# Attention and two MoE layers in one kernel: masked scores to SBUF, exponential in place, and another price list for the operation planner

## The chip, the cores and the metric

The kernel runs on one core of one Trainium2 chip. The metric is the device time of one execution in microseconds (us); the median of three runs stands for a kernel. Engines are named as in the profile: PE is the tensor engine, PEld its weight loads, DVE the vector engine, ACT the scalar engine, POOL is GpSimd, SP the queue that issues most DMAs.

## The reference

Everything is fp32. Attention has 4 batches, 8 heads, 576 positions and head size 64; its result becomes 2304 tokens of width 512 and passes through two MoE-like layers.

```
scores = q @ k^T / 8;  decay[i,j] = cum[i] - cum[j],  cum = cumsum(log(clip(f)))
s = where(j > i, -1e9, scores + decay);  s -= max(s)
attn = exp(s);  attn /= sum(attn) + 1e-9;  x = attn @ v        # 2304 x 512
h = x @ w1_in (512 x 2048);  x = (h * sigmoid(1.702 h)) @ w1_out
h = x @ w2_in;               out = (max(h,0) + alpha*min(h,0)) @ w2_out
```

## The kernel before

Every matmul operand is split into a high and a low fp32r half, so that a product takes three matmuls. The work is cut into operations ("ops"), and the kernel does not issue them in the order of the source: `plan.add` records an op with the engines it may use and what each would cost, and `Plan.plan` then simulates the whole kernel with those costs and picks, step by step, the op that could start first. [...]

**The planner's rules for PE.** Each PE op has a `mode`, meant to be the form in which the 128x128 array is used. An op whose mode differs from the one before it is charged `SWITCH` ns. When candidates are compared, an op of another mode counts as starting `pen` ns later than it could, unless it has been ready for `hold_for` ns already; ops of the first MoE product ("gemm1", `back`, priority 1000 and above) count as starting at least `back` ns later. `TRIES` lists the triples (pen, hold_for, back); each is planned and the plan with the earliest last start is used. `LAT` (230 ns) is added between engines. `pad` puts filler matmuls (L484) where the plan leaves PE idle in the first 130 us.

**The attention.** There are 16 pairs of heads (4 batches, 4 pairs each). A pair has two chunks of queries, 0 to 255 and 256 to 575. `chunk` computes a chunk's scores: for each tile of 128 queries and each head one PSUM bank, filled by matmuls with 64 rows (L878, mode 1; the two heads share the array), and for the last 64 queries of both heads by full-array matmuls (L872, mode 0). A DVE pass (L891, with a read of its accumulator) adds the mask, scales by -1/8 and takes the row minimum; an ACT pass (L900) takes the exponential and its row sum. Then come a small add (L909 or L905), the reciprocal (L911) and the scaling of the row (`a_scale`, L919 on DVE or POOL, L917 on ACT). `chunk2` transposes the scaled rows on PE by 128x128 blocks against the identity (L952), copies them out of PSUM (L513 ACT, L515 DVE, tiles `eT`) and multiplies by v (L966, half the array's columns per head, mode 2). `chunk2` of a chunk is added after `chunk` of the next one.

Per head pair there are ten passes L891 and ten exponentials, 160 of each in all: for each of the row lengths 128, 256, 288, 384 and 512, 32 of them.

**Buffers.** Eight PSUM banks are shared; scores may hold 3 at a time, the transposes 3, the v products 1, gemm1 2, the loads' transposes 2. In SBUF the rows of a tile lie in `ea`, `eb`, `ec`, `ed` (views `view[t, i]`, two buffers each), the transposed rows in `eT` (`ET` buffers of 640 columns), a pair's q in `QA` (`QS` buffers of two times 576).

**What runs beside it.** Once a block of tokens is finished, its share of gemm1 (L1008) can fill PE at low priority; what is left of it runs after the attention. Later come a tail of gemm1 in a seven-product scheme (L1031), the second product (L1252), and the second layer (the same scheme, L1434).

Of the kernel before, what the change touches and what calls it, by code (L numbers as in the profile page):

```python
# [23 lines left out]
QLAG = 3000.0  # L24
QPRI = 109.0
SLAG = 1000.0
SWITCH = 105.0
TMODE = 2
PADC = 8000.0
PAD0, PAD1, PADN, PADM = 1600.0, 130000.0, 220.0, 200.0  # L30
TRIES = [(60.0, 600.0, 400.0), (60.0, 300.0, 400.0)]
QUEUE = {"SP": "SP", "ACTQ": "ACT"}


# [215 lines left out]
def kernel(  # L250
# [45 lines left out]
    KEPT = 4  # L296
    HF = 256

    EB, ET, QS = 2, 4, 3
    SC_D, SC_A, SC_P = 0.0, 0.0, 0.0  # L300
    A0 = 100.0
    plan = Plan()
# [196 lines left out]
    def c_dve(n, fast=False):  # L499
        return n / (1.92 if fast else 0.96) + 68.0  # L500
# [206 lines left out]
    def load_qk(src, b, h0, w, c0, pri, actq):  # L707

        raw, T = Buf(p_raw), Buf(p_tk)
        for o in range(0, P, 32):  # L710
            hh, e_ = o // 64, o // 32 % 2
            d_ = DMA(32 * w * 4 * 1.6)
            if actq:
                d_.append(("ACTQ", d_[0][1], 300.0))
            plan.add(d_, lambda e, hh=hh, e_=e_, o=o: E[e].dma_start(
                raw.ap[o:o + 32, 0:w].rearrange("p (n d) -> p n d", d=32),
                src[b, h0 + hh, c0:c0 + w, 32 * e_:32 * e_ + 32].rearrange("(n p) d -> p n d", p=32),
            ), (), [(raw, o)], pri, QLAG if pri < QPRI else 0.0)
        plan.add([("DVE", 1.25 * w + 85.0)], lambda e: nc.vector.transpose(T.ap[:, :w], raw.ap[:, :w]), [raw], [T], pri)  # L719
        return T  # L720

    def split(T, w, big, keys, pri):
# [108 lines left out]
        return max(n / 2.4 + 13.5, 111.0 if m > 64 else 57.0)  # L831

    def a_scale(n):
        return [("DVE", c_dve(n, True), SC_D, True), ("ACT", c_act(n) + 30.0, SC_A), ("POOL", 280.0 + 2.55 * n, SC_P, True)]

    def chunk(u, q0, q1, pri):
        kh, kl, dk, qh, ql, qo, z = (u[x] for x in ("kh", "kl", "dk", "qh", "ql", "qo", "z"))
        pr = lambda c: range(2 if c > SPLIT else 1)
        ms = Buf(p_ms)
        n = q1 - q0  # L840
        tiles = [(t, t * P, min(P, S - t * P)) for t in range(q0 // P, (q1 + P - 1) // P)]
        view, eb = {}, {}
        if not q0:
            e0 = Buf(p_e0)
        for j, (t, a, w) in enumerate(tiles):
            ext = a + w
            if not q0:
                eb[t] = e0
                for hh in range(2):
                    view[t, hh] = lambda c0, c1, o=2 * P * j + hh * ext: e0.ap[:, o + c0:o + c1]  # L850
            elif w == P:
                eb[t] = x = Buf((p_e2, p_e3)[j])
                for hh in range(2):
                    view[t, hh] = lambda c0, c1, x=x, hh=hh: x.ap[:, hh, c0:c1]
            else:
                eb[t] = x = Buf(p_e4)
                fe = filled("ed", p_e4)
                view[t, 0] = lambda c0, c1, x=x: x.ap[:, c0:c1]
            step = ext if ext <= 512 else ext // 2
            for c0 in range(0, ext, step):  # L860
                c1 = c0 + step
                if q0 or j == 0:
                    pms = [Buf(ps_s) for _ in range(2 if w == P else 1)]
                f0 = 0 if q0 else a

                def mm(e, pms=pms, a=a, w=w, c0=c0, c1=c1, f0=f0):
                    if w < P:
                        o = pms[0].ap[:, :c1 - c0]
                        zz = lambda i: z.ap[:, i].rearrange("p h c -> p (h c)")
                        l = [(zz(0), kh.ap[:, c0:c1]), (zz(0), kl.ap[:, c0:c1]), (zz(1), kh.ap[:, c0:c1]), (ones[:, 1], dk.ap[:, c0:c1])]  # L870
                        for i, (x, y) in enumerate(l):
                            nc.tensor.matmul(o, x, y, start=i == 0, stop=i == 3)  # L872
                        return
                    for i, (x, y) in enumerate(((qh, kh), (qh, kl), (ql, kh), (None, dk))):
                        for hh in range(2):
                            r = slice(64 * hh, 64 * hh + 64)
                            l = ones[r, 0, :w] if x is None else x.ap[r, a - qo:a - qo + w]
                            nc.tensor.matmul(pms[hh].ap[:, f0:f0 + c1 - c0], l, y.ap[r, c0:c1], start=i == 0, stop=i == 3, skip_group_check=True)  # L878

                rd = [*((x, p_) for x in (kh, kl) for p_ in pr(c1)), *((dk, (i, p_)) for i in range(2) for p_ in (range(2) if u["first"] else pr(c1))), b_one, *u["fdk"]]  # L880
                rd += [z] if w < P else [qh, ql]
                plan.add([("PE", (4.4 if w == P else 4.0) * c_mm(c1 - c0, P))], mm, rd, [(x, f0) for x in pms], pri, mode=1 if w == P else 0,
                    pad=(pms[0], lambda x=pms[0], f0=f0, n=min(P, c1 - c0): x.ap[:, f0:f0 + n], 4 if pri == A0 and j == 0 else 0))
                for i, pm in enumerate(pms):
                    col = 4 + (c0 > 0) if w < P else 2 * j + i
                    if w == P:
                        mk, m0 = mask, 3 * P - t * P + c0
                    else:
                        mk, m0 = (mask, 0) if c1 < ext else (mask2, 0)
                    first = (lambda col=col: ms.ap[:, col - 1:col]) if c0 else lambda: 1.0e38  # L890
                    plan.add([("DVE", c_dve(c1 - c0) + 20.0)], lambda e, pm=pm, c0=c0, c1=c1, mk=mk, m0=m0, col=col, f0=f0, first=first: nc.vector.tensor_tensor_reduce(  # L891
                        pm.ap[:, f0:f0 + c1 - c0], pm.ap[:, f0:f0 + c1 - c0], mk[:, m0:m0 + c1 - c0], -0.125, first(),
                        ALU.add, ALU.min, accum_out=ms.ap[:, col:col + 1],
                    ), [b_mask if mk is mask else b_mask2, *([(ms, ("m", col - 1))] if c0 else [])], [(pm, f0), (ms, ("m", col))], pri)
                    if w == P:
                        last.append((pm, t, i, 0, c1, f0, col, 6 + col))
                    else:
                        last.append((pm, t, 0, c0, c1, f0, 5, 10 + (c0 > 0)))
            for pm, t_, i, x0, x1, f0, mc, sc in last:
                plan.add([("ACT", c_act(x1 - x0, True) + 190.0)], lambda e, pm=pm, t_=t_, i=i, x0=x0, x1=x1, f0=f0, mc=mc, sc=sc: nc.scalar.activation(  # L900
                    view[t_, i](x0, x1), pm.ap[:, f0:f0 + x1 - x0], AF.Exp, scale=-1.0, bias=ms.ap[:, mc:mc + 1], accum_out=ms.ap[:, sc:sc + 1]
                ), [(pm, f0), (ms, ("m", mc)), *(fe if w < P else [])], [(eb[t_], (t_, i, x0)), (ms, ("s", sc))], pri)
            last.clear()
            if w < P:
                plan.add([("DVE", 75.0, 0.0, True)], lambda e: nc.vector.scalar_tensor_tensor(  # L905
                    ms.ap[:, 10:11], ms.ap[:, 10:11], 1e-9, ms.ap[:, 11:12], op0=ALU.add, op1=ALU.add
                ), [(ms, ("s", 11))], [(ms, ("s", 10))], pri)
            else:
                plan.add([("DVE", 70.0, 0.0, True)], lambda e, j=j: nc.vector.tensor_scalar_add(ms.ap[:, 6 + 2 * j:8 + 2 * j], ms.ap[:, 6 + 2 * j:8 + 2 * j], 1e-9), (), [(ms, ("s", 6 + 2 * j)), (ms, ("s", 7 + 2 * j))], pri)  # L909
            cs = [6 + 2 * j, 7 + 2 * j] if w == P else [10]  # L910
            plan.add([("DVE", 85.0)], lambda e, cs=cs: nc.vector.reciprocal(ms.ap[:, cs[0]:cs[-1] + 1], ms.ap[:, cs[0]:cs[-1] + 1]), (), [(ms, ("s", c)) for c in cs], pri)  # L911
            for i, c in enumerate(cs):
                ks = [(eb[t], (t, i, x)) for x in range(0, ext, step)]
                def sc_(e, t=t, i=i, c=c, ext=ext):
                    x = view[t, i](0, ext)
                    if e == "ACT":
                        nc.scalar.mul(x, x, ms.ap[:, c:c + 1])  # L917
                    else:
                        E[e].tensor_scalar_mul(x, x, ms.ap[:, c:c + 1])  # L919
                plan.add(a_scale(ext), sc_, [(ms, ("s", c))], ks, pri)  # L920
        return dict(u=u, q0=q0, q1=q1, pri=pri, view=view, eb=eb)
# [3 lines left out]
    def chunk2(x):  # L925
# [5 lines left out]
        for t in range(nt):  # L931
# [27 lines left out]
            def av(e, et=et, t=t, s0=s0, m=m, w=w):  # L959
# [9 lines left out]
                    )  # L969
                    seen.add(hh)  # L970

            plan.add([("PE", max(4 * m / 2.4, 230.0) + 30.0)], av, [vr, et, *u["fvr"]], [pb], pri, mode=2,
                pad=(pb, lambda: pb.ap[:, :P], 0) if t == 0 else None)
        t0 = col0(b, q0)
        x = t0
# [530 lines left out]
```

## Time and profile before

| | |
|---|---|
| median of 3 runs | 969.73 us (969.11 to 970.33) |
| the profiled execution | 968.71 us, its span 967.0 us |
| PE busy over the span | 98% |
| DVE, ACT, POOL busy | 77%, 58%, 5% |
| granted TensorE clock | 0.999 of full speed |
| attention stretch | about the first 300 us |

The span runs from the first to the last instruction; 1.71 us of the execution's own time lie around it. The busy share of PE contains time in which matmuls are in flight but none is issued, so 98% is not 98% of its peak. Shares of busy time are averages over stages with different limits.

### The profile page before, as it was taken

What the parts mean: (1) busy time and instruction counts of PE and PEld (TensorE: products, weight loads), DVE (VectorE), ACT (ScalarE), POOL (GpSimd) and SP (SyncE); (2) the same over time, 40 slices, a digit from 0 to 9 for tenths busy, and PEclk for the clock granted to TensorE, in tenths of its full rate; (3) what the DMA queues carried; (4) which work ended last, traced back from release to release, by engine and by line L of the source; (5) the groups of instructions that cost most, each with busy time, mean ns of one, the idle gap of its engine ahead of it and who ended that gap; (6) DMA issues with size and microseconds to landing.
All of it is one profiled execution on the core that took longest, in us unless ns stands there. A gap on an engine that the chain in (4) does not pass through costs nothing.

```text
span 967.0 us, 18109 instructions
## 1 busy us (share of the span) xinstructions
PE 948.4 (98%) x6513; PEld 870.1 (90%) x6513; DVE 747.4 (77%) x1759; ACT 564.7 (58%) x1240; POOL 46.8 (5%) x56
## 2 busy tenths in 40 slices
PE   8999999999999999999999999999999999999998
PEld 5788887778889999988888988999999999999998
DVE  5999988888758029937657895888668978988987
ACT  6998977666564247757667784566455733221212
POOL 1112101010000003100000000000000000000000
PEclk9999999999999999999999999999999999999999
DMA  7868563432112247757887685678729495453523
GB/s 148 181 177 199 159 159 77 80 77 64 55 36 87 89 151 221 226 165 258 304 307 273 218 267 180 227 289 288 283 103 341 153 388 184 142 153 109 153 77 99
DMA packets 179035, 172.78 MB, mean 179 GB/s; under 512 B 98320, under 2 KB 153760, under 8 KB 176640
## 3 DMA queue, kind: packets, MB, share of 16 engines
q1 hardware_dynamic: 178928, 171.61, 57.3%
q8 instruction: 51, 0.84, 0.4%
q14 instruction: 40, 0.33, 0.1%
q10 hardware_dynamic: 16, 0.01, 0.0%
HBM read 107.71 MB, written 63.85 MB: 177 GB/s over the span
## 4 chain that ended last, share of the span: by engine, by line
PE 84%; DVE 11%; ACT 2%; DMA 2%; issue 1%; SPq 1%; DVEq 0%; ACTq 0%
PE bk L1031 23%; PE bk L1252 20%; PE bk L1434 19%; PE bk L1008 10%; PE bk L966 4%; PE bk L878 3%; DVE bk L891 3%; PE bk L952 3%; PE bk L872 2%; DVE ea L919 1%; DVE ec L919 1%; ACT ea L900 1%; DVE eT L515 1%; DVE tk L719 1%; DVE wc L688 1%
## 5 line engine op out<-in xcount | busy, mean ns | idle before, releaser
L1031 PE MATMUL bk<-x,wS 128*128 128x384 f32 x912 | 160.5, 335 | 0.3 <-DVE lx L1057 0.3
L1031 PEld LDWEIGHTS bk<-x,wS 128*128 128x128 f32 x912 | 158.1, 188 | 1.1 <-DVE lx L1057 0.8
L1252 PE MATMUL bk<-lh,w 128*128 128x512 f32 (+1 forms) x640 | 146.8, 368 | 0.0
L1008 PE MATMUL bk<-xh,w 128*128 128x320 f32 (+2 forms) x640 | 145.2, 307 | 0.2 <-DVE w L518 0.2
L1252 PEld LDWEIGHTS bk<-lh,w 128*128 128x128 f32 x640 | 112.8, 189 | 19.9
L1008 PEld LDWEIGHTS bk<-xh,w 128*128 128x128 f32 x640 | 108.3, 189 | 4.9 <-issue 2.6
L1008 PE MATMUL bk<-xl,w 128*128 128x320 f32 (+2 forms) x320 | 97.0, 303 | 0.0
L518 DVE TENSOR_TENSOR ll<-lx,lh 128x512 fp32r<-128x512 f32 (+1 forms) x80 | 50.9, 636 | 49.8 <-PE bk L1252 41.6
L1252 PE MATMUL bk<-ll,w 128*128 128x512 f32 (+1 forms) x320 | 81.2, 368 | 0.0
L891 DVE CUSTOM_DVE_ANT_0 bk<-bk,mask 128x128 f32<-128x128 f32 (+4 forms) x144 | 68.1, 498 | 16.6 <-PE bk L878 13.7
L513 ACT CAST x<-x 128x768 fp32r<-128x768 f32 (+3 forms) x41 | 33.4, 825 | 67.7 <-PE bk L1434 55.2
L1434 PE MATMUL bk<-wS,x 128*128 128x256 f32 x567 | 70.5, 283 | 0.0
L1434 PEld LDWEIGHTS bk<-wS,x 128*128 128x128 f32 x567 | 69.1, 192 | 0.0
L1434 PE MATMUL bk<-wS,lh 128*128 128x256 f32 x378 | 68.7, 283 | 0.0
L1218 ACT ACTIVATE lx<-lx 128x512 f32<-128x512 f32 (+1 forms) x80 | 46.9, 587 | 37.0 <-DVE ll L518 31.3
L1252 PEld LDWEIGHTS bk<-ll,w 128*128 128x128 f32 x320 | 57.1, 189 | 9.8
L1008 PEld LDWEIGHTS bk<-xl,w 128*128 128x128 f32 x320 | 60.4, 189 | 0.0
L513 ACT CAST lh<-x 128x768 fp32r<-128x768 f32 (+3 forms) x29 | 23.2, 806 | 63.3 <-PE bk L1434 48.6
L518 DVE TENSOR_TENSOR x<-x,x 128x768 fp32r<-128x768 f32 (+3 forms) x59 | 55.9, 980 | 4.1 <-ACT x L513 3.1
L1434 PEld LDWEIGHTS bk<-wS,lh 128*128 128x128 f32 x378 | 59.0, 192 | 0.0
L513 ACT COPY lx<-bk 128x384 f32<-128x384 f32 x72 | 34.2, 480 | 39.3 <-PE bk L1031 25.1
L1434 PE MATMUL bk<-wS,ll 128*128 128x256 f32 x189 | 53.5, 283 | 0.0
(200 smaller groups left out, 1982.3 us busy)
## 6 DMA issues: line engine op xcount, KB each, us to landing
h2scr<-lx SPq DMA_DIRECT2D x96, 192.0 KB
wraw<-in_moe_w_in_dram SPq DMA_DIRECT2D x32, 512.0 KB
wraw<-in_moe_w_out_dram SPq DMA_DIRECT2D x32, 512.0 KB
lx<-h1scr SPq DMA_DIRECT2D x64, 256.0 KB
x<-h2scr SPq DMA_DIRECT2D x32, 512.0 KB
w2scr<-wS SPq DMA_DIRECT2D x5, 1792.0 KB
tscr<-wS SPq DMA_DIRECT2D x4, 1792.0 KB
wS<-tscr SPq DMA_DIRECT2D x4, 1792.0 KB
```

The lines of the kernel that those rows point to most:

```text
L513: nc.scalar.copy(dst, src)
L518: E[e].tensor_tensor(dst, a, b, op=ALU.subtract)
L872: nc.tensor.matmul(o, x, y, start=i == 0, stop=i == 3)
L878: nc.tensor.matmul(pms[hh].ap[:, f0:f0 + c1 - c0], l, y.ap[r, c0:c1], start=i == 0, stop=i == 3, skip_group_check=True)
L891: plan.add([("DVE", c_dve(c1 - c0) + 20.0)], lambda e, pm=pm, c0=c0, c1=c1, mk=mk, m0=m0, col=col, f0=f0, first=first: nc.vector.tensor_te ...
L952: nc.tensor.transpose(pt.ap[:, i * P:(i + 1) * P], view[j, hh](t * P, t * P + P), ident)
L966: nc.tensor.matmul(pb.ap[64 * hh:64 * hh + 64, x0:x1], vr.ap[:, t, hh], et.ap[:, c0:c0 + x1 - x0], start=t == 0 and hh not in seen, stop=t ...
L1008: nc.tensor.matmul(ph.ap[:, :n], w.ap[:, a, c, :], x[c // 2].ap[:, c % 2, :n], start=(c == 0 and j == 0), stop=(c == KT - 1 and j == 2))
L1031: nc.tensor.matmul(out.ap[:, :XH], wt(a, c), x.ap[:, b, c, :], start=(st and c == 0 and i == 0), stop=(c == 1 and i == 2), skip_group_chec ...
L1218: plan.add([("ACT", c_act(n))], lambda e: nc.scalar.activation(g.ap[:, :n], raw.ap[:, :n], AF.Gelu_apprx_sigmoid), [raw], [g], pri)
L1252: nc.tensor.matmul(py[d].ap[:, :n], w[:, a, d * P:(d + 1) * P], (lo if x else h).ap[:, :n], start=(k == 0 and (a, x) == (0, 0)), stop=(k = ...
L1434: nc.tensor.matmul(py[j].ap[:, t * HF:(t + 1) * HF], x.ap[:, q:q + P], w[:, o, a, :], start=(k == 0 and t == 0 and c == 0), stop=(k == NPA ...
```

## The change

Three things are done. The masked scores are written by L891 into the SBUF rows, not back into their PSUM bank, and the exponential reads those rows and writes over them; the bank is no longer an operand of the exponential. The planner's list is altered: transposes count as mode 0 (with gemm1 and the other full-array matmuls) and not as mode 2, a change costs 180 ns and not 105, the one triple is (800, 3000, 200) in place of (60, 600, 400) and (60, 300, 400), and several costs differ (lower for L719's transpose, for L878's scores and L966's products, higher for the scalings, 42 ns higher for the exponential). And there are 6 `eT` buffers in place of 4, and 2 `QA` buffers in place of 3. No instruction is added and none is dropped, except that the number of fillers follows from the plan.

```diff
-SWITCH = 105.0
-TMODE = 2
+SWITCH = 180.0
+TMODE = 0
-TRIES = [(60.0, 600.0, 400.0), (60.0, 300.0, 400.0)]
+TRIES = [(800.0, 3000.0, 200.0)]
-    EB, ET, QS = 2, 4, 3
+    EB, ET, QS = 2, 6, 2
...
-        plan.add([("DVE", 1.25 * w + 85.0)], lambda e: nc.vector.transpose(T.ap[:, :w], raw.ap[:, :w]), [raw], [T], pri)
+        plan.add([("DVE", 1.04 * w + 92.0)], lambda e: nc.vector.transpose(T.ap[:, :w], raw.ap[:, :w]), [raw], [T], pri)
...
-        return [("DVE", c_dve(n, True), SC_D, True), ("ACT", c_act(n) + 30.0, SC_A), ("POOL", 280.0 + 2.55 * n, SC_P, True)]
+        return [("DVE", c_dve(n, True) + 62.0, SC_D, True), ("ACT", c_act(n) + 105.0, SC_A), ("POOL", 280.0 + 2.55 * n, SC_P, True)]
...
-                plan.add([("PE", (4.4 if w == P else 4.0) * c_mm(c1 - c0, P))], mm, rd, [(x, f0) for x in pms], pri, mode=1 if w == P else 0,
+                plan.add([("PE", 4 * c_mm(c1 - c0, P))], mm, rd, [(x, f0) for x in pms], pri, mode=1 if w == P else 0,
...
-                    plan.add([("DVE", c_dve(c1 - c0) + 20.0)], lambda e, pm=pm, c0=c0, c1=c1, mk=mk, m0=m0, col=col, f0=f0, first=first: nc.vector.tensor_tensor_reduce(
-                        pm.ap[:, f0:f0 + c1 - c0], pm.ap[:, f0:f0 + c1 - c0], mk[:, m0:m0 + c1 - c0], -0.125, first(),
+                    plan.add([("DVE", c_dve(c1 - c0) + (69.0 if c0 else 10.0))], lambda e, pm=pm, i=i, t=t, c0=c0, c1=c1, mk=mk, m0=m0, col=col, f0=f0, first=first: nc.vector.tensor_tensor_reduce(
+                        view[t, i](c0, c1), pm.ap[:, f0:f0 + c1 - c0], mk[:, m0:m0 + c1 - c0], -0.125, first(),
                         ALU.add, ALU.min, accum_out=ms.ap[:, col:col + 1],
-                    ), [b_mask if mk is mask else b_mask2, *([(ms, ("m", col - 1))] if c0 else [])], [(pm, f0), (ms, ("m", col))], pri)
+                    ), [(pm, f0), b_mask if mk is mask else b_mask2, *([(ms, ("m", col - 1))] if c0 else []), *(fe if w < P else [])], [(eb[t], (t, i, c0)), (ms, ("m", col))], pri)
...
-            for pm, t_, i, x0, x1, f0, mc, sc in last:
-                plan.add([("ACT", c_act(x1 - x0, True) + 190.0)], lambda e, pm=pm, t_=t_, i=i, x0=x0, x1=x1, f0=f0, mc=mc, sc=sc: nc.scalar.activation(
-                    view[t_, i](x0, x1), pm.ap[:, f0:f0 + x1 - x0], AF.Exp, scale=-1.0, bias=ms.ap[:, mc:mc + 1], accum_out=ms.ap[:, sc:sc + 1]
-                ), [(pm, f0), (ms, ("m", mc)), *(fe if w < P else [])], [(eb[t_], (t_, i, x0)), (ms, ("s", sc))], pri)
+            for t_, i, x0, x1, mc, sc in last:
+                plan.add([("ACT", c_act(x1 - x0) + 190.0)], lambda e, t_=t_, i=i, x0=x0, x1=x1, mc=mc, sc=sc: nc.scalar.activation(
+                    view[t_, i](x0, x1), view[t_, i](x0, x1), AF.Exp, scale=-1.0, bias=ms.ap[:, mc:mc + 1], accum_out=ms.ap[:, sc:sc + 1]
+                ), [(ms, ("m", mc))], [(eb[t_], (t_, i, x0)), (ms, ("s", sc))], pri)
...
-            plan.add([("PE", max(4 * m / 2.4, 230.0) + 30.0)], av, [vr, et, *u["fvr"]], [pb], pri, mode=2,
+            plan.add([("PE", max(4 * m / 2.4, 230.0))], av, [vr, et, *u["fvr"]], [pb], pri, mode=2,
```

## Rows read from the trace of the kernel before

**Rows 1.** The page: the span.

```profile
span 967.0 us, 18109 instructions
```

**Rows 2.** Busy time by stage: PE, PEld, DVE, ACT, POOL, clock, DMA share, GB/s.

```profile
30.00:300.00 270.00, 260.61 (x2209) 220.43 (x2208) 234.49 (x754) 203.03 (x563) 31.26 (x26) 1.00 0.47 112
300.00:345.00 45.00, 45.00 (x279) 45.00 (x279) 12.25 (x22) 13.72 (x27) 0.00 (x0) 1.00 0.28 96
345.00:967.00 622.00, 617.71 (x3847) 586.55 (x3845) 482.31 (x896) 326.58 (x589) 11.24 (x12) 1.00 0.64 215
```

**Rows 3.** The chain of waits, 120 to 300 us: start, us, what.

```profile
169.68 2.25 PE bk L966 x24
...
185.29 2.25 PE bk L966 x24
...
288.66 11.34 PE bk L1008 x76
```

**Rows 4.** PE in order of time, one head pair: start, us, instruction, [idle before].

```profile
177.54 0.31 PE L1008 MATMUL bk<-xh,w 128*128 128x320 f32 x1
177.78 0.55 PE L878 MATMUL bk<-KA,QA 64*128 64x128 f32 x6
...
178.90 0.42 PE L1008 MATMUL bk<-xh,w 128*128 128x320 f32 x1
...
180.86 0.80 PE L878 MATMUL bk<-KA,QA 64*128 64x384 f32 x6
...
181.76 0.33 PE L952 MATMUL bk<-ident,eb 128*128 128x128 f32 x1
...
185.22 2.32 PE L966 MATMUL bk<-eT,VR 128*64 128x320 f32 x28
187.47 0.87 PE L952 MATMUL bk<-ident,ea 128*128 128x128 f32 x6
188.27 0.96 PE L878 MATMUL bk<-KA,QA 64*128 64x512 f32 x6
...
189.40 0.67 PE L872 MATMUL bk<-KA,Z 128*128 128x288 f32 x3
...
190.13 0.87 PE L966 MATMUL bk<-eT,VR 128*64 128x256 f32 x8
190.93 0.67 PE L872 MATMUL bk<-KA,Z 128*128 128x288 f32 x3
```

**Rows 5.** Waits of PE, 30 to 300 us: waited for, us in total, times, longest.

```profile
PE bk L952 <- DVE eT L515: 3.6, 5, 0.8
PE bk L952 <- ACT ea L900: 2.0, 2, 1.1
```

**Rows 6.** Waits of PE's weight loads, 30 to 300 us.

```profile
PEld bk L952 <- ACT ea L900: 3.5, 6, 1.4
```

**Rows 7.** ACT by line and shape, to 290 us: count | busy us, mean ns | idle before.

```profile
L900 ACT ACTIVATE ec<-bk,ms 128x512 f32<-128x512 f32 x32 | 22.2, 695 | 15.7 <-DVE ms L891 14.3 <-DVE ms L909 1.4
...
L900 ACT ACTIVATE ea<-bk,ms 128x128 f32<-128x128 f32 x32 | 11.7, 368 | 13.0 <-DVE ms L891 13.0
...
L917 ACT ACTIVATE ec<-ec,ms 128x512 f32<-128x512 f32 x6 | 4.3, 724 | 1.4 <-DVE ms L911 1.3
...
L917 ACT ACTIVATE ea<-ea,ms 128x128 f32<-128x128 f32 x10 | 4.1, 421 | 0.2 <-DVE ms L911 0.2
```

**Rows 8.** DVE by line and shape, 30 to 300 us.

```profile
L891 DVE CUSTOM_DVE_ANT_0 bk<-bk,mask 128x512 f32<-128x512 f32 x32 | 21.9, 704 | 6.6 <-PE bk L878 6.6
...
L515 DVE COPY eT<-bk 128x512 f32<-128x512 f32 x4 | 2.7, 680 | 0.3 <-PE bk L952 0.3
```

**Rows 9.** POOL, DVE and PE in order of time, 177 to 193 us.

```profile
182.69 1.40 POOL L518 TENSOR_TENSOR QA<-tk,QA 128x576 fp32r<-128x576 f32 x1 [14.21 <-ACT QA L513]
...
182.92 1.33 DVE L919 TENSOR_SCALAR ea<-ea,ms 128x256 f32<-128x256 f32 x1
...
184.64 0.33 PE L952 MATMUL bk<-ident,ec 128*128 128x128 f32 x1 [0.76 <-DVE eT L515]
```

More of the change, by code (lines that the diff above doesn't have):

```diff
@@ L890, in chunk @@
                     first = (lambda col=col: ms.ap[:, col - 1:col]) if c0 else lambda: 1.0e38
-                    plan.add([("DVE", c_dve(c1 - c0) + 20.0)], lambda e, pm=pm, c0=c0, c1=c1, mk=mk, m0=m0, col=col, f0=f0, first=first: nc.vector.tensor_tensor_reduce(
-                        pm.ap[:, f0:f0 + c1 - c0], pm.ap[:, f0:f0 + c1 - c0], mk[:, m0:m0 + c1 - c0], -0.125, first(),
+                    plan.add([("DVE", c_dve(c1 - c0) + (69.0 if c0 else 10.0))], lambda e, pm=pm, i=i, t=t, c0=c0, c1=c1, mk=mk, m0=m0, col=col, f0=f0, first=first: nc.vector.tensor_tensor_reduce(
+                        view[t, i](c0, c1), pm.ap[:, f0:f0 + c1 - c0], mk[:, m0:m0 + c1 - c0], -0.125, first(),
                         ALU.add, ALU.min, accum_out=ms.ap[:, col:col + 1],
-                    ), [b_mask if mk is mask else b_mask2, *([(ms, ("m", col - 1))] if c0 else [])], [(pm, f0), (ms, ("m", col))], pri)
+                    ), [(pm, f0), b_mask if mk is mask else b_mask2, *([(ms, ("m", col - 1))] if c0 else []), *(fe if w < P else [])], [(eb[t], (t, i, c0)), (ms, ("m", col))], pri)
                     if w == P:
-                        last.append((pm, t, i, 0, c1, f0, col, 6 + col))
+                        last.append((t, i, 0, c1, col, 6 + col))
                     else:
-                        last.append((pm, t, 0, c0, c1, f0, 5, 10 + (c0 > 0)))
-            for pm, t_, i, x0, x1, f0, mc, sc in last:
-                plan.add([("ACT", c_act(x1 - x0, True) + 190.0)], lambda e, pm=pm, t_=t_, i=i, x0=x0, x1=x1, f0=f0, mc=mc, sc=sc: nc.scalar.activation(
-                    view[t_, i](x0, x1), pm.ap[:, f0:f0 + x1 - x0], AF.Exp, scale=-1.0, bias=ms.ap[:, mc:mc + 1], accum_out=ms.ap[:, sc:sc + 1]
-                ), [(pm, f0), (ms, ("m", mc)), *(fe if w < P else [])], [(eb[t_], (t_, i, x0)), (ms, ("s", sc))], pri)
+                        last.append((t, 0, c0, c1, 5, 10 + (c0 > 0)))
+            for t_, i, x0, x1, mc, sc in last:
+                plan.add([("ACT", c_act(x1 - x0) + 190.0)], lambda e, t_=t_, i=i, x0=x0, x1=x1, mc=mc, sc=sc: nc.scalar.activation(
+                    view[t_, i](x0, x1), view[t_, i](x0, x1), AF.Exp, scale=-1.0, bias=ms.ap[:, mc:mc + 1], accum_out=ms.ap[:, sc:sc + 1]
+                ), [(ms, ("m", mc))], [(eb[t_], (t_, i, x0)), (ms, ("s", sc))], pri)
             last.clear()
```

## The prediction

> **What bounds the kernel now.** I read the page first, for the span of 967.0 us [rows 1] and for PE, which it shows busy nearly throughout; but a busy PE is not one that issues all the time. The table by stage then says where the change can act. From 345 us on, PE is busy 617.71 of 622 us, on work that is neither attention nor in another array form [rows 2]; nothing of the diff touches it, and I leave it as it is. From 300 to 345 us PE has no idle time at all [rows 2]. What runs there is the rest of gemm1: the chain shows it from 288.66 us, 76 matmuls in 11.34 us, 0.149 us each [rows 3]. That rest decides how everything else is read: gemm1 is a store of PE work that can fill a hole in the attention whenever its tokens exist. With some 45 us of it left over, the attention's latency is free, and the end of the stretch is set by the sum of what PE does up to 345 us: useful matmuls, changes of array form, and waits. A microsecond less of the last two is a microsecond less in the end; a later attention chunk costs nothing until the store is empty.
>
> The reader is to see three kinds of loss in 30 to 300 us. First, plain idle time of PE: 270 − 260.61 = 9.4 us [rows 2]. Second, what it waits for: 3.6 us of transposes (L952) behind copies of eT by DVE, and 2.0 us of transposes behind exponentials (L900) that still hold a PSUM bank [rows 5]. Third, changes of array form, which the busy time hides. The chain repeats every 15.61 us, from one run of 24 v products at 169.68 to the next at 185.29 [rows 3]; this is one head pair, and 12 of the 16 pairs (batches 1 to 3) go like it. Within one period PE goes full array, scores, full, scores, transposes (full), v products, transposes, scores, L872 (full), v products, L872: ten changes [rows 4]. One costs about 0.09 us: gemm1's last matmul starts at 177.54, the scores at 177.78, 0.24 us later [rows 4], against the usual 0.149 [rows 3]. I use 0.1. Ten per period in 12 periods are 12 us.
>
> DVE is busy 234.49 of 270 us, ACT 203.03 [rows 2]. They are not the bound, but DVE is near enough for a late DVE to be seen on PE.
>
> **The change, part by part.**
>
> (a) *Banks freed by the masked pass.* The exponential no longer reads the bank, so the waits of the transposes for an exponential go. That is 2.0 us of PE [rows 5]. Below it lies nothing (the bank may then be waited for behind L891 on a busy DVE); above it the 3.5 us that the weight loads ahead of the same transposes wait [rows 6]. I take −2.0, the matmuls' own idle time. The next thing late there is DVE's masked pass, which has to run before the exponential anyway.
>
> (b) *Fewer changes of form.* Before, the planner thought that going between transposes and v products was free, while a period has two such borders (185.22, 187.47) [rows 4], and that gemm1 next to transposes cost something. With transposes in mode 0 its modes are the array's forms, and `pen` 800 for up to 3000 ns makes it stay in a form. The least a period needs is four (into scores and out, into v products and out); with three score banks and one chunk's lag it will not get there. Six `eT` buffers let all five blocks of the second chunk be transposed before their products; four did not. I take seven changes instead of ten: 3 × 0.1 × 12 = −3.6 us. Bounds: 0, and six fewer, −7.2 us.
>
> (c) *Transposes that wait for copies.* The 3.6 us behind eT copies are waits inside runs of transposes [rows 5]. gemm1 may now go between transposes without a charge, and is put back by 200 ns instead of 400. I take half, −1.8 us, with bounds 0 and −3.6.
>
> (d) *Planned waiting.* The same `pen` makes the planner leave PE idle for up to 0.8 us rather than change the form, if an op of the present form comes ready within that time and everything else has been ready for less than 3 us. No row shows this, since before the value was 60 ns. At least it costs nothing; one full 0.8 us wait for each of seven changes in a period would be 5.6 us, 67 us in all. I take a value near the low end, because gemm1's store is nearly always a candidate of full-array form, and while PE is in that form nothing idles: one wait of 0.25 us per period, 12 × 0.25 = +3.0 us. For the range I let it go to +14.
>
> (e) *Exponential from SBUF.* The nearest row is ACT's scaling, the same engine from and to SBUF with a pointer operand: 724 ns for 512 columns against 695 for the exponential from PSUM, 421 against 368 for 128 [rows 7]. So each exponential is longer by 29 to 53 ns, about 40, and 160 of them add 6.4 us of ACT. ACT's idle quarter covers it (67 us in 30 to 300 us); with the cover gone it would be all 6.4. I take +0.5.
> [...]
>
> (f) *Masked pass into SBUF.* Nearest row: DVE's copy from PSUM to SBUF takes 680 ns for 512 columns, the masked pass within PSUM 704 [rows 8]. 24 ns × 160 = 3.8 us less DVE, of which I put −0.3 on PE. [...]
>
> (g) *Costs and buffers.* The new costs for scalings, transposes, scores and products change no instruction, only the order; I cost them at nothing. One `QA` buffer less: K's buffers are two as well and turn over with the same pair, so q waits no longer than k does. SP's and ACT's DMA queues get no new transfer. If that cover is gone, one late pair costs a few tenths of a us in each period; this lies within (d)'s upper bound.
>
> Sum: −2.0 − 3.6 − 1.8 + 3.0 + 0.5 − 0.3 = **−4.2 us**. The profiled execution took 968.71 us (span 967.0, 1.71 around it), so 964.5; the median of the runs lies 1.02 above that execution, so **965.5 us**.
>
> **Rivals.**
>
> *Nothing measurable.* The holes that (a) to (c) close are found again at another wait: DVE is 87% busy, and a transposed row still needs mask, exponential, scaling and copy. For it: the losses are small pieces, and the order of every engine is reshuffled. Against it: gemm1 can fill. Time: 967.8 to 971.7 (0.2% either way is about what a measurement of this kernel can tell from no change), say 969.5.
>
> *Slower, by planned waiting.* As in (d), but with more of it. It decides when the waiting exceeds (a) to (c), 7.4 us, or 0.62 us per period: one nearly full hold in each pair. At 1.2 us per period it is 14.4 − 7.4 = +7, that is 977. For it: 0.8 us is eight times what one change costs [rows 4], so the planner pays too much to avoid one. Against it: gemm1 that has been ready for 3 us is not held.
>
> *Slower, by the port.* The masked pass now writes SBUF while POOL works there. What such a meeting costs is seen once in a period [rows 9]: a scaling on DVE, begun at 182.92 while POOL's subtraction runs (182.69 to 184.09), lasts 1.33 us, and the copy of eT and the transpose after it are late by 0.76 us. One more of these in each period would be 12 × 0.76 = 9.1, less 4.2: +4.9, 974.6. Against it: the copies from PSUM to SBUF are near the masked pass in time [rows 8].
> [...]
>
> *Larger gain.* (a), (b) and (c) at their upper bounds without (d): −3.5 − 7.2 − 3.6 + 0.2 = −14.1, 955.6.
>
> **How the numbers follow.** Forecast 0.45 (960 to 967.8), larger gain 0.12, nothing measurable 0.19, planned waiting 0.20, the port 0.04. Faster by over 0.2%: 0.45 + 0.12 = 0.57; within: 0.19; slower: 0.24. The range runs from 956, which leaves about 0.06 below (half of the larger gain), to 976, which leaves about 0.11 above (half of the planned waiting). The forecast's own range is 960 to 967.8.
>
> **What would show it.** (a): no wait of L952 or L878 for L900 in 30 to 300 us. (b): seven or fewer changes in a period of PE's timeline; v products in longer runs. (c): less waiting of L952 for L515. (d): idle PE without a releaser that matches a PSUM bank, ahead of L878 or L966. (e), (f): exponentials near 735 ns for 512 columns, masked passes near 680. All of it must come out before the tail of gemm1 begins; the stretch after 345 us must keep its length. The prediction is wrong if the attention's period is no shorter while gemm1's rest after it is as long as before, or if PE idles more than 9.4 us in the attention.

## The result: 952.7 us, 1.7% faster, four times the gain that was forecast

The changed kernel takes 952.73 us (951.22 to 955.17), before 969.45 on the same chip: the ratio is 0.9829 (0.9802 to 0.9855). That is 16.7 us; the forecast was 4.2, and its range ended at 956. The nearest of the rivals was the larger gain (955.6). One execution of a_tmode22, below, took 1145.3 us at a granted clock of 0.75 and is left out of its median.

The page and the table by stage of the changed kernel, with the columns of [rows 2]:

```profile
span 949.6 us, 18126 instructions
```

```profile
0.00:30.00 30.00, 26.41 (x186) 19.75 (x187) 17.88 (x85) 20.03 (x55) 3.88 (x18) 0.94 0.77 165
30.00:300.00 270.00, 267.89 (x2328) 238.82 (x2326) 224.59 (x764) 209.36 (x585) 23.28 (x23) 1.00 0.49 117
300.00:345.00 45.00, 45.00 (x263) 45.00 (x262) 30.20 (x57) 21.61 (x40) 2.53 (x3) 1.00 0.43 145
345.00:949.00 604.00, 600.57 (x3747) 569.42 (x3745) 467.15 (x867) 310.18 (x560) 1.47 (x2) 1.00 0.63 215
```

PE idles 2.1 us of 30 to 300 (9.4 before), and issues 2328 matmuls there in place of 2209: the same work, packed closer, so that all that follows starts earlier. The last v product starts at 285 us (288 before), and 288 of gemm1's matmuls are left after it (384 before). The waits of PE in that stretch, to be held against [rows 5]:

```profile
PE bk L952 <- DVE eT L515: 1.0, 1, 1.0
PE bk L878 <- DMA KB<-cscr: 0.5, 1, 0.5
PE bk L1008 <- DVE xl L518: 0.4, 1, 0.4
```

How the holes of the transposes went can be seen in order of time, in a pair of the changed kernel that does not look like [rows 4]:

```profile
183.75 0.27 PE L952 MATMUL bk<-ident,eb 128*128 128x128 f32 x1
183.86 0.27 PE L952 MATMUL bk<-ident,ec 128*128 128x128 f32 x1
183.97 0.27 PE L952 MATMUL bk<-ident,ed 128*128 128x128 f32 x1
184.00 0.36 PE L1008 MATMUL bk<-xh,w 128*128 128x256 f32 x1
...
184.68 0.28 PE L1008 MATMUL bk<-xh,w 128*128 128x256 f32 x1
184.80 0.27 PE L952 MATMUL bk<-ident,eb 128*128 128x128 f32 x1
...
187.19 0.88 PE L952 MATMUL bk<-ident,ea 128*128 128x128 f32 x6 [1.02 <-DVE eT L515]
187.82 0.37 PE L1008 MATMUL bk<-xh,w 128*128 128x256 f32 x1
```

gemm1 (L1008) stands between two groups of transposes and costs no change of form: it starts 0.03 us after the last transpose (184.00 after 183.97), and the next transpose 0.12 us after its last matmul (184.80 after 184.68). One idle stretch of PE behind an eT copy is left between 30 and 300 us, the 1.02 us that end at 187.19.

The best ledger is not idle time but time from one matmul's start to the next one's, added up by the line of the first. Over both traces the sums differ by 17.4 us, and the transposes have nearly all of it: 400 of them took 60.8 us before and 45.1 after, where 400 x 0.11 us (their steady spacing, 183.75 to 183.86 to 183.97 above) are 44. The scores (L878) gave 2.0, L872 1.3, the v products 1.1; gemm1 took 1.3 more, the fillers 1.0. The changes of form, counted where two matmuls in a row differ in rows or columns, fell from 176 to 133.

The 15.7 us of the transposes are of three kinds. From one transpose to the next, 365 steps took 14.0 us more than 0.11 each before, and 368 took 2.8 more after: these are waits, 11.3 us fewer. A change of form followed a transpose 30 times before and twice after: 2.7 us. The remaining 1.7 are no gain: where gemm1 follows, it starts 0.03 us after the transpose, and the time stands in gemm1's sum instead.

### The profile page after: what moved, and what is told of

Read it like the earlier page. It is cut to its first block, busy times and chain, and to the rows that moved or that the text cites. A ratio compares the mean times of both kernels' runs of the same rounds, so it can differ in the third digit from the quotient of the medians.

```text
span 949.6 us, 18126 instructions
## 1 busy us (share of the span) xinstructions
PE 939.9 (99%) x6517; PEld 873.0 (92%) x6517; DVE 739.8 (78%) x1771; ACT 561.2 (59%) x1238; POOL 31.2 (3%) x46
## 4 chain that ended last, share of the span: by engine, by line
PE 89%; DVE 5%; DMA 1%; issue 0%; ACT 0%; DVEq 0%; SPq 0%; ACTq 0%
PE bk L1031 25%; PE bk L1252 21%; PE bk L1434 19%; PE bk L1008 12%; PE bk L966 4%; PE bk L952 4%; PE bk L878 3%; PE bk L872 1%; DVE w L518 1%; DVE wc L688 1%; DMA raw<-in_k_dram 1%; DVE eT L515 0%; DVE wc L687 0%; DVE tk L719 0%; DVE eb L891 0%
## 5 line engine op out<-in xcount | busy, mean ns | idle before, releaser
L1031 PE MATMUL bk<-x,wS 128*128 128x384 f32 x912 | 160.4, 334 | 0.0
L1031 PEld LDWEIGHTS bk<-x,wS 128*128 128x128 f32 x912 | 158.2, 188 | 0.7 <-DVE lx L1057 0.5
L1008 PE MATMUL bk<-xh,w 128*128 128x320 f32 (+2 forms) x640 | 150.2, 310 | 0.1
L1252 PE MATMUL bk<-lh,w 128*128 128x512 f32 (+1 forms) x640 | 146.9, 368 | 0.0
L1252 PEld LDWEIGHTS bk<-lh,w 128*128 128x128 f32 x640 | 112.7, 189 | 19.8
L1008 PEld LDWEIGHTS bk<-xh,w 128*128 128x128 f32 x640 | 108.9, 189 | 4.5 <-issue 1.7
L1008 PE MATMUL bk<-xl,w 128*128 128x320 f32 (+2 forms) x320 | 97.0, 303 | 0.4 <-DVE xl L518 0.4
L518 DVE TENSOR_TENSOR ll<-lx,lh 128x512 fp32r<-128x512 f32 (+1 forms) x80 | 50.9, 636 | 40.0 <-PE bk L1252 26.1
L1252 PE MATMUL bk<-ll,w 128*128 128x512 f32 (+1 forms) x320 | 81.2, 368 | 0.0
L1434 PE MATMUL bk<-wS,x 128*128 128x256 f32 x567 | 70.5, 283 | 0.0
L1434 PEld LDWEIGHTS bk<-wS,x 128*128 128x128 f32 x567 | 69.1, 192 | 0.0
L1434 PE MATMUL bk<-wS,lh 128*128 128x256 f32 x378 | 68.7, 283 | 0.0
L1252 PEld LDWEIGHTS bk<-ll,w 128*128 128x128 f32 x320 | 57.0, 189 | 9.6
L1008 PEld LDWEIGHTS bk<-xl,w 128*128 128x128 f32 x320 | 60.5, 189 | 0.7 <-DVE xl L518 0.7
L518 DVE TENSOR_TENSOR x<-x,x 128x768 fp32r<-128x768 f32 (+3 forms) x59 | 55.9, 979 | 4.1 <-ACT x L513 3.1
L1434 PEld LDWEIGHTS bk<-wS,lh 128*128 128x128 f32 x378 | 59.0, 192 | 0.0
L1434 PE MATMUL bk<-wS,ll 128*128 128x256 f32 x189 | 53.5, 283 | 0.0
L513 ACT CAST lh<-lx 128x512 fp32r<-128x512 f32 (+1 forms) x68 | 38.9, 572 | 16.8 <-PE bk L1252 16.3
```

The lines of the kernel that those rows point to most:

```text
L513: nc.scalar.copy(dst, src)
L518: E[e].tensor_tensor(dst, a, b, op=ALU.subtract)
L1008: nc.tensor.matmul(ph.ap[:, :n], w.ap[:, a, c, :], x[c // 2].ap[:, c % 2, :n], start=(c == 0 and j == 0), stop=(c == KT - 1 and j == 2))
L1031: nc.tensor.matmul(out.ap[:, :XH], wt(a, c), x.ap[:, b, c, :], start=(st and c == 0 and i == 0), stop=(c == 1 and i == 2), skip_group_chec ...
L1252: nc.tensor.matmul(py[d].ap[:, :n], w[:, a, d * P:(d + 1) * P], (lo if x else h).ap[:, :n], start=(k == 0 and (a, x) == (0, 0)), stop=(k = ...
L1434: nc.tensor.matmul(py[j].ap[:, t * HF:(t + 1) * HF], x.ap[:, q:q + P], w[:, o, a, :], start=(k == 0 and t == 0 and c == 0), stop=(k == NPA ...
```

## The experiments

Two names first. The *rules* of a kernel are its prices, modes, buffers and the place of its scores; an *order* is what the planner makes of them, the sequence in which the instructions of each engine are issued. Every experiment but one gets a new order of nearly all instructions, and that turned out to matter as much as the rules. In the table, "changes" and "L952" are counted as above (L952: us from start to start, all 400), "last v" is the start of the last v product.

| kernel | median us | changes | L952 us | last v us |
|---|---|---|---|---|
| before | 969.5 | 176 | 60.8 | 288 |
| b_nudge, b_nudge2: before, latency 236, 222 | 962.8, 960.0 | 163, 163 | 53.3, 53.5 | 290, 284 |
| b_sbuf: before + scores in SBUF | 962.8 | 168 | 53.8 | 282 |
| b_tmode: before + transposes as mode 0 | 962.9 | 165 | 53.3 | 287 |
| b_modes, b_modes2: before + modes and prices | 969.7, 967.5 | 143, 145 | 56.4, 54.6 | 333, 326 |
| b_sbuf_modes, b_sbuf_modes2: both | 958.7, 961.8 | 139, 139 | 49.6, 49.2 | 296, 298 |
| a_psum, a_psum2: changed, scores in PSUM | 961.8, 960.6 | 143, 139 | 50.6, 49.0 | 323, 316 |
| a_tmode2, a_tmode22: changed, transposes as mode 2 | 958.8, 959.5 | 159, 154 | 50.5, 52.7 | 287, 285 |
| a_price: changed, old prices | 959.3 | 159 | 48.1 | 278 |
| a_cost: changed, old costs | 961.2 | 138 | 50.6 | 291 |
| a_buf: changed, old buffers | 960.0 | 142 | 47.3 | 301 |
| a_nudge, a_nudge2: changed, latency 236, 222 | 959.9, 955.7 | 139, 132 | 47.2, 44.5 | 296, 294 |
| changed | 952.7 | 133 | 45.1 | 285 |

**One part from each end.** The theories: filling (gemm1 between transposes) against banks (the exponential lets go of the bank).

b_sbuf adds to before the L891 and L900 lines of the diff, with the two ops' new costs; a_psum takes them out of the changed kernel. The lines as b_sbuf changes them:

```diff
-                        pm.ap[:, f0:f0 + c1 - c0], pm.ap[:, f0:f0 + c1 - c0], mk[:, m0:m0 + c1 - c0], -0.125, first(),
+                        view[t, i](c0, c1), pm.ap[:, f0:f0 + c1 - c0], mk[:, m0:m0 + c1 - c0], -0.125, first(),
...
-                    view[t_, i](x0, x1), pm.ap[:, f0:f0 + x1 - x0], AF.Exp, scale=-1.0, ...
+                    view[t_, i](x0, x1), view[t_, i](x0, x1), AF.Exp, scale=-1.0, ...
```

> The kernel before with one part of the change: masked scores into SBUF, exponential in place there, with the two new costs of these ops; modes, prices, other costs and buffers as before. Filling theory (what counts is that transposes are in gemm1's mode, so that gemm1 fills the holes in runs of transposes): about 2 us faster than before, near 967.5 us. Bank theory (what counts is that the exponential lets go of the bank): most of the 16.7 us, 956 us or less, and the waits of transposes in 30 to 290 us, 7.9 us of PE idle before, fall to about 1 us.

> The changed kernel with the masked scores back in their PSUM bank and the exponential reading them there (and their two old costs); everything else as changed. Filling theory: 2 to 4 us slower than the changed kernel, 955 to 957. Bank theory: near the kernel before, 965 or more.

b_tmode sets the transposes' mode alone, as below; a_tmode2 sets it back to 2 in the changed kernel:

```diff
-TMODE = 2
+TMODE = 0
```

> The kernel before with transposes as mode 0 in place of mode 2, nothing else. Filling theory: at least half of the 16.7 us, 961 us or less, with some 20 places where gemm1 follows transposes on PE (none before). Bank theory: within 3 us of before, 967 to 972.

> The changed kernel with transposes as mode 2 again, everything else as changed. Filling theory: 8 us slower than the changed kernel or more, 961 or more. Bank theory: within 3 us of it, 950 to 956.

All four missed both theories: 962.8, 961.8, 962.9, 958.8. From before (970.3 us on the chip of these runs) either part seemed to give some 7.5 us, from the changed kernel either seemed to be worth 6 to 9. In b_tmode gemm1 followed a transpose only 6 times, not 20 (the triple's `pen` and `back` were unchanged), and the time fell all the same. That two unlike parts gave the same time and nearly the same L952 sum called for a null experiment.

**The draw.** Only the planner's latency is nudged, in either kernel:

```diff
-LAT = 230
+LAT = 236        # 222 in the second of each
```

> The kernel before with the planner's latency between engines 236 ns in place of 230, nothing else: another order of nearly all instructions from the same rules. If single parts of the change gained some 7.5 us each because their mechanisms work, this is within 2 us of before, 968 to 972. If the order of before is only an unlucky draw which any new order leaves (luck theory), it gains like the parts did: 960 to 966.

> As the last, with 222 ns in place of 230. Mechanism theory: 968 to 972. Luck theory: 960 to 966.

> The changed kernel with the latency 236 ns in place of 230. Mechanism theory: within 2 us of it, 951 to 955. Luck theory (the changed kernel's order is a lucky draw as well): 957 to 963.

> As the last, with 222 ns in place of 230. Mechanism theory: 951 to 955. Luck theory: 957 to 963.

Nudged, the rules of before gave 962.8 (ratio 0.9928, 0.9913 to 0.9943) and 960.0 (0.9905); the changed rules 959.9 (0.990) and 955.7 (0.9853). Three of the four are as the luck theory had it; a_nudge2 lies between the two. So the order of before was a poor draw and that of the changed kernel a good one. The means of three are 964.1 and 956.1, 8 us apart, but the three values on each side scatter so much (4.8 and 3.6 us of standard deviation) that the 8 have a standard error of 3.5 and are not clear of zero. The pair at 230 ns is also the one whose difference is to be explained; the nudged pairs alone differ by 2.9 and 4.3 us. So **some 4 to 8 us of the 16.7 belong to the rules, as far as these draws tell**, and at least half to the two draws. b_sbuf and b_tmode, 962.8 and 962.9, are no better than a nudge. What does not overlap between the sides: 163 to 176 changes against 132 to 139, and 53 to 61 us of L952 against 45 to 47. The waits from transpose to transpose, 14.0 us in before, are 6.9 and 6.6 in its nudged orders, and 2.8, 4.3 and 2.6 in the changed ones: the nudge alone took half of them away.

**Is POOL the fault of the poor draw?** The meeting of [rows 9] comes back in period after period: in before, scalings of 256 columns that begin at 151.7, 167.4, 182.9, 198.5 and 214.2 us, each beside an L518 of POOL, last 1.28 to 1.35 us. b_acts keeps the order of before and issues the DVE scalings of 256 columns on ACT:

```diff
+            if eng == "DVE" and o in MOVE:      # MOVE: the scalings of 256 columns
+                eng = "ACT"
             o.fn(eng)
```

> The order of before, kept instruction by instruction, with one difference: where the plan puts the scaling of a 256-column row on DVE, it is issued on ACT at the same place of the order. In before, ten scalings on DVE last over 0.8 us because POOL's subtraction runs, nine of them once in each head pair. Collision theory (the order of before is slow because it meets POOL in every period, and the transposes wait for the copies queued behind that scaling): 5 to 8 us faster than before, 962 to 965, and the 0.76 us wait of the transposes for eT copies goes from the periods. Rival (the wait has another cause, and ACT's longer scaling only shifts it): within 2 us of before.

968.9 us, ratio 0.9987 (0.9977 to 0.9997): the collision theory falls as a cause of the whole. The chains of before and of b_acts show what it is worth (five lines added to the source make L966 L971):

```profile
138.40 2.25 PE bk L966 x24
...
216.54 2.25 PE bk L966 x24
```

```profile
141.32 2.25 PE bk L971 x24
...
171.41 2.25 PE bk L971 x24
186.48 2.25 PE bk L971 x24
...
216.64 2.25 PE bk L971 x24
```

The period is 15.07 us against 15.61 [rows 3], so the collision cost some 0.5 us in each of the five regular periods from 141 to 217 us, 2.8 us together (b_acts' products start 2.9 us late at 141 us and 0.1 us late at 217). But b_acts had lost as much before: 2.0 us by 35 us, 2.9 by 124. Nine of the seventeen scalings lie there, and ACT is nearly full (81.7 of the 90 us from 30 to 120 in before); but the granted clock from 0 to 300 us was also lower, 0.99 where before had 1.00, and the run does not separate the two. What else made the order of before poor is not settled.

**Prices, and prices with banks.** b_modes sets SWITCH, TMODE and TRIES as changed; b_sbuf_modes adds the scores in SBUF; a_price undoes SWITCH and TRIES alone. b_modes2, b_sbuf_modes2, a_psum2 and a_tmode22 have the latency 222.

```diff
-SWITCH = 105.0
-TMODE = 2
-TRIES = [(60.0, 600.0, 400.0), (60.0, 300.0, 400.0)]
+SWITCH = 180.0
+TMODE = 0
+TRIES = [(800.0, 3000.0, 200.0)]
```

> The kernel before with the three forms and their prices as changed (transposes as mode 0, 180 ns a change, the one triple), other costs, buffers and scores as before. Two nudged orders of before gave 960 and 963 us, with 163 changes of form. If the prices carry the gain beyond the draw: 954 to 958 us and at most 140 changes. If they need the freed banks or the other costs: 959 to 965 us.

> The kernel before with the three forms and their prices as changed, latency 222 ns: a second draw beside 969.7 us and 143 changes. If the prices alone gain nothing: 960 to 970, at most 145 changes, and more waiting of transposes than in the changed kernel. If the first was a bad draw: 953 to 958.

> The changed kernel with 105 ns a change and the two old triples, transposes still as mode 0, the rest as changed. If the prices and the long hold carry the gain: 959 to 965 us and 155 or more changes of form. If the freed banks and the mode of the transposes do it alone: 953 to 958 us.

> The changed kernel with masked scores back in PSUM, and the planner's latency 222 ns in place of 230: a second draw beside the 961.8 us of the first. The changed scores gave 952.7, 955.7 and 959.9 us with three latencies, mean 956.1. If the freed banks are worth 4 us or more: 960 to 965. If they are worth nothing: 953 to 959.

> The kernel before with the forms' prices and the masked scores in SBUF; other costs and buffers as before. Together theory (a planner that stays longer in a form needs the banks freed early): 953 to 960, near the changed kernel's three draws (mean 956.1). Rival (the other costs or the eT buffers are needed too): 961 or more.

> As the last, with latency 222 ns, a second draw. Together theory: 953 to 960. Rival: 961 or more.

> The changed kernel with transposes as mode 2, latency 222 ns: a second draw beside 958.8. If the transposes' mode is worth 4 us: 958 to 962 and about 159 changes. If nothing: 953 to 957.

The prices alone gave 969.7 and 967.5 us: fewer changes (143 and 145) and no gain. 969.7 lies outside both ranges that were named. Their mean, 968.6, is 7 us above the nudged before and 4.5 above the mean of its three draws. With the scores in SBUF too, 958.7 and 961.8: 6 to 11 us better than the prices alone at the same latency, though the second meets the rival's "961 or more" and not the 953 to 960 of the theory. From the other end a_psum and a_psum2 gave 961.8 and 960.6, where the changed rules have a mean of 956.1. So under the new prices the scores' place is worth some 5 to 8 us: taken together, four orders have a mean of 964.9 and five one of 957.8, 7.1 us apart with a standard error of 2.7. That the prices add to the scores' place is not shown: against b_sbuf (962.8) the two runs with both gain 1 to 4 us, and a_price, with the old prices in the changed kernel, gave 959.3 and 159 changes, as its first theory had it, but a_nudge was 959.9 with no part undone. The transposes' mode is in the same state: a_tmode2 and a_tmode22 (958.8, 959.5) lie 3 us above the mean of the changed rules, within the scatter of the draws.

Where the scores stay in PSUM and the planner holds, the attention drags on (last v at 316 to 333 us in four kernels, 285 to 301 in the seven with the same prices and mode and the scores in SBUF). The v products of b_modes, then of b_sbuf_modes (count, min/median/max ns, first and last start):

```profile
L966 PE MATMUL bk<-eT,VR x544: 219/326/796, 45.0 to 333.4; 128*64 128x256 f32 x57, 128*64 128x320 f32 x45, 128*64 128x64 f32 x38, 128*64 128x128 f32 x27
```

```profile
L966 PE MATMUL bk<-eT,VR x544: 219/300/483, 50.4 to 295.6; 128*64 128x256 f32 x57, 128*64 128x320 f32 x45, 128*64 128x64 f32 x38, 128*64 128x128 f32 x27
```

The last one starts at 333 us, not 296. After it only 90 of gemm1's matmuls are left in b_modes, 258 in b_sbuf_modes: the store that was to fill the holes is nearly used up, and the waits of PE in b_modes, 30 to 340 us, include gemm1's own for its operands:

```profile
PE bk L952 <- DVE ed L919: 2.2, 1, 2.2
PE bk L952 <- ACT gg L513: 2.1, 1, 2.1
...
PE bk L1008 <- DVE xl L518: 0.8, 1, 0.8
PE bk L1008 <- DVE w L518: 0.7, 2, 0.5
```

That the banks are what delays it is argued, not shown. In three kernels with their scores in SBUF (changed, a_nudge, b_sbuf_modes) no transpose waits for an exponential, in six with PSUM scores 2 (b_nudge2) to 18 (b_acts) of these waits are seen; but the same edit takes some 12 us of work off DVE (last section), and transposes wait for DVE's copies as well (8.7 us behind L515 in before). No run gave the old scores more banks, or DVE the same relief without the banks.

**The rest.** a_cost and a_buf undo the other costs, and the buffers:

```diff
-        plan.add([("DVE", 1.04 * w + 92.0)], ...            # a_cost, with the scalings',
+        plan.add([("DVE", 1.25 * w + 85.0)], ...            # scores' and products' costs
...
-    EB, ET, QS = 2, 6, 2                                    # a_buf
+    EB, ET, QS = 2, 4, 3
```

> The changed kernel with the old costs of transposes on DVE, scalings, scores and products. If truer costs make the last 4 us: 960 or more, with more waiting of transposes than in the changed kernel. If not: 952 to 959.

> The changed kernel with 4 eT and 3 QA buffers. If the eT buffers make the last 4 us: 960 or more, and 145 or more changes of form. If not: 952 to 959 and about 135 changes.

961.2 and 960.0 us. Taken by its total a_cost would confirm its part, and a_buf stands on its border (its 142 changes are neither the 145 that were named for it nor the 135 against it); but a_nudge was 959.9 with no part undone, and one draw each can't tell them from it. Their L952 sums are 50.6 and 47.3 against 44.5 to 47.2 for the changed rules: the truer costs may count for the transposes, the buffers less; this stays open.

## Why the prediction was wrong, point by point

**The bound was right.** All of the gain lies in lines that run during the attention; the three that follow (L1031, L1252 and L1434) add up to 612.6 us from start to start in both kernels. PE's sum of work, changes and waits sets the end.

**(a) and (c), the waits of the transposes: mis-sized, the step that failed.** I took 2.0 + 1.8 = 3.8 us out of PE's own idle time in [rows 5]. From transpose to transpose before lost 14.0 us in waits, and 11.3 of them went. Two things were left out. The rows used are two of five; the other three, in the same view of before, are

```profile
PE bk L952 <- ACT ed L917: 1.5, 1, 1.5
PE bk L952 <- DVE ed L919: 0.5, 1, 0.5
...
PE bk L952 <- ACT eT L513: 0.3, 1, 0.3
```

And idle time is only part of the loss. A matmul counts as busy while it is in flight (0.27 us each here, at a spacing of 0.11), so the first 0.16 us of a wait between two of them leave no idle time on PE: of the 14.0 us, 8.0 are idle time and 6.0 are hidden in this way. The waits show more fully at the weight loads, of which I used only the row with the exponential [rows 6]. The longest waits of both engines at L952 by releaser, 30 to 300 us, in the changed kernel:

```profile
  DVE eT L515: 2.3, 2
  DVE ms L911: 0.7, 2
  DVE ms L891: 0.4, 1
```

and in the kernel before:

```profile
  DVE eT L515: 8.7, 11
  ACT ea L900: 5.5, 8
  ACT ed L917: 3.5, 3
  ACT eT L513: 2.5, 8
```

The mechanisms named are there: the waits for an exponential are gone (no L900 in the changed kernel, 5.5 before), and gemm1 follows a transpose 23 times, where it did so once before. But how much of the 11.3 us is theirs is another matter: nudging before, with no part of the change, took 7 us of these waits away, and between the nudged kernels the difference is 3.3 us, about what I wrote.

**(g), "only the order, costed at nothing": the other step that failed.** A change of 3% in one price moves the time by 3 to 10 us here. The forecast had no term for the draw, and the range should have been wider by some 5 us to each side for that alone. Against the means over three draws, 8 us apart, the forecast of 4.2 is about half; against the nudged pairs, 2.9 and 4.3 us, it has the size. That the measured gain is four times as large is the luck of the two draws for the greater part.

**(b), fewer changes: right.** Eight in a pair of the changed kernel (177.4 to 197.0 us) where seven were forecast, 176 to 133 in all; 43 x 0.1 us = 4.3 us, where −3.6 was written (2.7 of them are already counted in the transposes' 15.7). I had 12 regular pairs; the chain of before has five regular periods (138 to 217 us). The larger gain lies in the waits of the transposes, not here, and b_modes shows that the prices which make changes fewer gain nothing by themselves.

**(d), planned waiting: seen, but not in the changed kernel.** There PE idles 2.1 us, and the +3.0 that was written did not come. With the scores in PSUM the same prices are 4.5 us slower than the mean of before's draws and 7 slower than its nudged ones: the rival's sign, its place not quite (waits at transposes and at gemm1, not idle PE ahead of scores).

**(e) and (f): right on ACT, short on DVE.** Exponentials of the changed kernel, with the columns of [rows 7]:

```profile
L900 ACT ACTIVATE ec<-ec,ms 128x512 f32<-128x512 f32 x32 | 23.2, 730 | 2.9 <-DVE ms L891 2.9
...
L900 ACT ACTIVATE ea<-ea,ms 128x128 f32<-128x128 f32 x32 | 12.7, 396 | 4.4 <-DVE ms L891 4.3
```

730 and 396 ns are 35 and 28 more than from PSUM [rows 7]. The estimate of about 40, from ACT's scalings [rows 7], has the sign and is somewhat high. The masked pass:

```profile
L891 DVE CUSTOM_DVE_ANT_0 ec<-bk,mask x32: 665/685/692, 34.7 to 272.5; 128x512 f32<-128x512 f32 x32
L891 DVE DVE_READ_ACCUMULATOR2_ANT ms<- x160: 71/82/89, 15.9 to 274.6; 128x1 f32 x160
```

685 ns against 704 [rows 8]; 680 was written. Over all 160 passes that is 3.1 us of DVE, where 3.8 was written. But the read of its accumulator, which I had not costed, fell too (below). What either is worth on PE no run separates.

**The port rival did not occur.** None of the 32 passes of 512 columns took more than 692 ns; three of them ran beside a POOL instruction, in 680 to 687 ns. A scaling of 256 columns beside POOL's L518 still took 1.50 us there (at 185.17). Whether a port or something else sets the two apart, no run shows; the chance of 0.04 was my estimate.

## What to carry to other kernels

Size the loss of an engine whose instructions overlap in flight by the time from start to start, per line, against the steady spacing; its idle time showed 8 of the 14 us here. Where a planner or scheduler makes the order, nudge a price that should not matter, on both kernels, before any part is credited: here the draw was at least as large as what is left for the rules, and single-part experiments read without it would each have "explained" 7 us. And a price that makes one engine wait for longer runs did not pay by itself: prices alone gave some 20 changes fewer than a nudge and no time, and with the scores out of PSUM they were 8 us better than that. Whether it is the buffers freed early or the work taken off DVE stays open.

## What was not expected of the hardware

The accumulator read behind the masked pass took 139 ns (mean of 160) when the pass wrote to PSUM, and 82 when it wrote to SBUF. In these four kernels it goes with the scores' place alone: medians of 141 in before, 140 in a_psum, 81 in b_sbuf, 82 in the changed kernel. That is 57 ns x 160 = 9.1 us of DVE, more than the 3.1 us that the pass itself gained; together some 12 us.

In the first 30 us the granted clock of the changed kernel is 0.94 (0.83 from 20 to 30 us, after PE had stood for 1.09 us until 19.6 and 0.38 until 20.3, waiting for k), where before kept 1.00 although PE had stood longer there, 2.10 us until 20.6. In the first 30 us b_nudge shows 0.89, b_modes, b_modes2, b_sbuf_modes2 and a_psum 0.94, b_nudge2 and b_sbuf_modes 1.00. No run isolates what that costs.
